# Retention attention and a squared-ReLU FFN on one core: four value loads on a second DMA queue, a new load order, other fillers

## The chip, the cores and the metric

The kernel runs on one core of a Trainium2 chip. A core has five engines that run side by side and wait for each other through semaphores: TensorE (PE, matrix products into PSUM), VectorE (DVE), ScalarE (ACT), GpSimd (POOL) and SyncE (SP, which here only issues DMA transfers). Weight loads of TensorE are listed apart as PEld. Sixteen DMA engines move data between HBM and SBUF; they are fed from queues of the issuing engines. The metric is the device time of one execution in microseconds, the median over several runs. The profile is taken from one execution; its span runs from the first to the last instruction.

## The reference

Two stages follow each other. The first is a recurrent attention with a decay per head; the second is an FFN with a squared ReLU.

```python
# q, k, v: (4, 8, 768, 64) f32; gamma_h = 1 - 2**(-5 - h)
for t in range(S):
    state = gamma * state + outer(k[:, :, t], v[:, :, t])
    y[:, :, t] = q[:, :, t] @ state / sqrt(D)
x = y.transpose(0, 2, 1, 3).reshape(3072, 512)
h = maximum(x @ w_in, 0)            # w_in 512 x 2048
out = (h * h) @ w_out               # w_out 2048 x 512, out 3072 x 512 f32
```

## The kernel before

The 3072 tokens are worked in 24 chunks of 128 tokens, six for each of four batches (`where(m)` gives batch and place). All eight heads of a chunk are worked together.

For each chunk `m`, `prepare(m)` loads k, q and v (256 KB each, in rows of 64 floats) into one of four staging slots, casts k and q to bf16, and scales v while casting it (L366). `transpose(m)` turns k and q, so that the head dimension lies on partitions: by TensorE through a PSUM bank (`T`, L408, with an eviction by ACT or DVE) for `m < NPE`, by small TensorE flips inside a visit (L381, one eviction at L387) for `NPE <= m < NTD`, and by a DMA transpose (L399) for the rest. `visit` holds the attention products of TensorE: scores (L451) and the chunk's own k-v sums (L462) for one chunk, values (L425) and the application of the state (L440) for another. DVE masks the scores (L505), updates the states (L516, L518) and writes the product with the decay factors to the activation tile `xt` (L527).

The FFN weights come in eight transfers of 1 MB: `i0` to `i3` are column quarters of w_in, `o0` to `o3` row quarters of w_out. They share four f32 staging buffers `wst`: `o0` uses the one of `i0`, and so on, so that a quarter of w_out can be loaded only when the casts of the same quarter of w_in are done. Each quarter is cast to bf16 in four slices, spread over DVE, ACT and POOL (`copy_on`, L341 to L345).

`ffn1(blk)` multiplies a block of one, two or four chunks (`BLOCKS`) with w_in: groups of 16, 8 or 4 matmuls of 128, 256 or 512 columns fill one of four PSUM banks `fps` (L565); ACT takes the ReLU (L570), DVE squares (L575). A group needs all chunks of its block and one quarter of w_in. `ffn2(blk)` multiplies each chunk's hidden layer with w_out (L608): 16 matmuls of 512 columns, in four pieces of four, one for each quarter of w_out, into one bank; at most two such groups are open at a time. ACT evicts the result (L616) and SyncE stores it (L620). Of the last chunk the output is worked in two halves of 256 columns.

The order of the instructions on all engines is made by a planner, `Plan.schedule`. It is a list scheduler with a model of durations: at each step it takes, over all engines, the operation that could start earliest, with the lowest `prio` among equals. The priority of a load is its place in the text `ORDER`; a store has -1, a DMA transpose -0.5. Operations with several possible engines (`CAST`, `WCAST`, `EVAC`) go where they start first. Loads are modelled as one shared pipe with a cost each (`SMALL`, `TURN`, `WIDE`, `STORE`), a number of descriptors against a ring limit of 198, and a time for which the issuing queue is held. The planned times only set the order; on the chip each instruction waits for its data.

TensorE gets filler matmuls that compute nothing used (L657): before each TensorE operation that is planned before `WARM`, as many as the planned idle time holds, times `FILL`. They write the last `fps` bank, which is withheld from other use until then. The priorities of F2 pieces contain `F2LAG`, in chunks, by which they stand behind the F1 groups.

All loads, transposes and stores are issued by SyncE.

Of the kernel before, what the change touches and what calls it, by code (L numbers as in the profile page):

```python
# [18 lines left out]
class Plan:  # L19
# [4 lines left out]


    DMA_LATENCY = 1.9
    LAND = 1.25
    RING = 198
    FETCH = 2.6
# [34 lines left out]
    def schedule(self, nbanks, max_open):  # L64
# [8 lines left out]
        start = [None] * n  # L73
        end = [None] * n
        eng_free = {}
        pool = {}
        for o in ops:
            for e in o["eng"]:
                eng_free.setdefault(e, 0.0)
                pool.setdefault(e, set())  # L80
                if left[o["i"]] == 0:
                    pool[e].add(o["i"])
        bank_free = [0.0] * (nbanks - 1) + [WARM]
        bank_of = {}
        open_groups = set()
        pipe = 0.0
        outstanding = {e: [] for e in eng_free}
        done = 0
        issued, edge, next_fetched, history, crossed = 0, self.BLOCK0, 3.0, [], 0.0
        while done < n:  # L90
            best = None
            for eng, cand in pool.items():
                ef = eng_free[eng]
                for i in cand:
                    o = ops[i]
                    t = max(ef, ready_at[i])
                    b = o["bank"]
                    if b is not None and b[0] == "open":
# [5 lines left out]
                        t = max(t, min(free))  # L104
# [5 lines left out]
            o = ops[i]  # L110
# [3 lines left out]
            dur = o["eng"][eng]  # L114
            move = isinstance(dur, tuple)
            if move:
                cost, n_desc, hold = dur
                out_ = outstanding[eng]
                while out_ and out_[0][0] <= t:
                    out_.pop(0)  # L120
                while sum(x[1] for x in out_) + n_desc > self.RING:
                    t = max(t, out_.pop(0)[0])
# [7 lines left out]
                    open_groups.add(b[1])  # L130
            if move:
                eng_free[eng] = t + hold
                pipe = max(pipe, t + self.DMA_LATENCY) + cost
                end[i] = pipe + self.LAND
                out_.append((pipe, n_desc))
                dur = hold
            else:
                if eng == "PE":
                    o["fill"] = 0
                    if t < WARM:  # L140
                        o["fill"] = int(max(0.0, t - max(eng_free[eng], 1.5) - 0.3) * FILL / 0.427)
                    issued += 2 * o["fill"]
                    todo, per = 2 * o["count"], dur / max(1, 2 * o["count"])
                    now = t
                    while issued + todo > edge:
                        step = max(0, edge - issued)
                        now = max(now + step * per, next_fetched)
                        issued, todo = max(issued, edge), todo - step
                        ahead = next((y for x, y in reversed(history) if x <= edge - self.AHEAD), 0.0)
                        ahead = max(ahead, crossed)  # L150
                        crossed = now
                        edge += self.BLOCK
                        next_fetched = ahead + min(5.7, max(0.3, pipe - ahead)) + self.FETCH
                    issued += todo
                    dur = now + todo * per - t
                    history.append((issued, t + dur))
                    o["dur"] = dur
                eng_free[eng] = t + dur
                end[i] = t + dur + o["lat"]
# [14 lines left out]
        return sorted(range(n), key=lambda i: (start[i], i))  # L174


SMALL = (1.20, 65, 0.6)
TURN = (1.10, 16, 2.4)
WIDE = (2.85, 33, 0.6)
STORE = (0.80, 9, 0.6)  # L180
BLOCKS = [1, 1, 1, 1, 1, 1, 2, 2, 2, 4, 4, 4]
SPLIT = 6
AHEAD = 4
WARM = 20.0
FILL = 0.8
PACE = 8
LEAD = 2
NPE = 6
NTD = 8
QACT = 0  # L190
F2LAG = 3.0
F2WAIT = 4
CAST = {"k": {"DVE": 0.43, "ACT": 0.63, "POOL": 0.78}, "q": {"DVE": 0.43, "ACT": 0.63, "POOL": 0.78}}
WCAST = {"DVE": 0.43, "ACT": 0.63, "POOL": 0.78}
# [2 lines left out]


ORDER = (
    "k0 q0 q1 v0 k1 q2 v1 k2 v2 v3 k3 q3 i0 i1 q4 o0 i2 i3 k4 o1 v4 o2 o3 v5 v6 q5 k5 q6 v7 q7 k6 k7"  # L200
)


# [8 lines left out]
def kernel(  # L212
# [9 lines left out]
    nc = tc.nc  # L222
    P = nc.NUM_PARTITIONS
# [22 lines left out]
    NBANK = 4  # L246
# [7 lines left out]
    ident = sb("ident", [P, P], BF16)  # L254
# [8 lines left out]
    ld = {x: sb(f"{x}n", [P, NLD, H * D], FP32) for x in "qkv"}  # L263
# [20 lines left out]
    pl = Plan()  # L284
# [63 lines left out]
    def prepare(m):  # L348
        b, i = where(m)
        slot = m % NLD  # L350
        for x in "kqv":
            t = ld[x][:, slot, :]
            side = x == "q" and m < QACT
            pl.add(f"ld{x}{m}", "ACT" if side else "SP", SMALL, (), (f"ld{x}{slot}",),
                   lambda x=x, t=t, q_=nc.scalar if side else nc.sync: q_.dma_start(  # L355
                       t.rearrange("s (h d) -> s h d", h=H),
                       src[x][b, :, i * C : (i + 1) * C, :].rearrange("h s d -> s h d")),
                   prio=dma_prio[(x, m)] - 200 * side)
        for x in "kq":
            t, o = ld[x][:, slot, :], bf[x][m % NBF]  # L360
            pl.add(f"c{x}{m}", CAST[x], 0, (f"ld{x}{slot}",), (f"bf{x}{m % NBF}",),
# [227 lines left out]
    def ffn2(blk):  # L589
        for q4 in range(blk0[blk], blk0[blk] + blocks[blk]):  # L590
# [5 lines left out]
            for part in range(parts):  # L596
# [4 lines left out]
                for j in range(4):  # L601
                    reads = [f"h{g % NH2}.{u}.{4 * j + c}" for c in range(4)] + [f"wout{j}.{c}" for c in range(4)]

                    def mm(j=j, o1=o1, h2=h2, u=u, ns=ns, w=w):
                        ps = fps[o1["op"]["bank_index"]]
                        for c in range(4):
# [1 line left out]
                            nc.tensor.matmul(ps[:, 0:w], lhsT=h2[:, fb, u * C : u * C + C], rhs=w_out_bf[j][:, c, ns],  # L608
                                             start=(fb == 0), stop=(fb == NFB - 1))
                    i0 = pl.add(f"F2.{q4}.{j}" + f"/{part}" * (parts > 1), "PE", 0.866 / parts, reads, (f"g{grp}",), mm,  # L610
                                prio=(q4 + F2LAG) * 8 + 2 * j + 1 + part * 0.5, lat=0.2,
                                bank=("open", grp, True) if j == 0 else ("use", grp), count=4)
                    if j == 0:
                        o1["op"] = pl.ops[i0]
# [37 lines left out]
    if tc is not None:  # L652
        with tc.manual_schedule():
            for i in sequence:
                o = pl.ops[i]
                for _ in range(o.get("fill", 0)):
                    nc.tensor.matmul(fps[NBANK - 1][:], lhsT=ident[:],  # L657
                                     rhs=ident[:, None, :].to_broadcast([P, 4, P]), start=True, stop=True)
                o["fn"](o["on"]) if o["flex"] else o["fn"]()
    return pl  # L660

# [29 lines left out]
```

## Time and profile before

| | |
|---|---|
| median of five runs | 215.99 us (214.99 to 216.83) |
| the profiled execution | 216.83 us |
| its span | 214.8 us |
| TensorE busy | 203.1 us, 95% |
| DVE, ACT, POOL busy | 53%, 41%, 20% |
| F1 matmuls (L565) | 768, 94.5 us busy |
| F2 matmuls (L608) | 400, 92.2 us busy |
| fillers (L657) | 12, 6.5 us busy |
| loads of k, q, v | 24 each, 256 KB each |
| weight loads | 8, 1 MB each, some 10.3 us from issue to landing |
| DMA transposes | 16 |

Busy times of TensorE overlap, since matmuls are pipelined: the busy sum is more than the time that the work takes in a row. In the list of pieces of the chain, each piece has its start, its length, engine, what and line. In the timeline, a line has start, length, engine, source line, operation, output and input, and in brackets how long the engine was idle before it and what ended that. A row of a stretch has the stretch, its length, the busy time and count of PE, PEld, DVE, ACT and POOL, the granted TensorE clock, the DMA share and the rate in GB/s. "SPq" is SyncE's queue, with the time in which it was occupied with issuing.

### The profile page before, as it was taken

The numbers are of one execution on the slowest core, as the hardware profiler recorded it, in microseconds if no ns is written. First come the engines' busy times: TensorE is split into PE (matmuls) and PEld (weight loads), VectorE is DVE, ScalarE is ACT, GpSimd is POOL, SyncE is SP. The second block draws the span as 40 slices with busy tenths as digits, with TensorE's granted clock in tenths as the row PEclk, the third lists the DMA queues.
The fourth block names the chain that finished last, engine by engine and source line by source line (L and its number), as shares of the span: only waits on it lengthen the run. The fifth ranks groups of instructions, "written<-read, shape, count | busy, mean of one in ns | idle before, by whom it ended". The sixth has DMA issues, their size and how long they took to land.

```text
span 214.8 us, 6317 instructions
## 1 busy us (share of the span) xinstructions
PE 203.1 (95%) x2764; PEld 121.2 (56%) x2764; DVE 113.1 (53%) x249; ACT 87.5 (41%) x145; POOL 42.1 (20%) x68
## 2 busy tenths in 40 slices
PE   6884899999999999999999999999999999999992
PEld 2453799776457787666754444454444444444461
DVE  1566767765149597675755665556554433322100
ACT  8222458735145254343331644223534324534211
POOL 5412323324331223132221223231100000000000
PEclk9999999999999999999999999999999999999999
DMA  7999999999899999989999999999811010011031
GB/s 142 216 203 331 352 348 319 346 244 231 203 268 187 190 182 194 236 194 210 236 199 236 206 218 167 221 202 170 153 50 52 3 63 34 3 49 49 28 112 56
DMA packets 99627, 38.15 MB, mean 178 GB/s; under 512 B 92304, under 2 KB 92560, under 8 KB 99600
## 3 DMA queue, kind: packets, MB, share of 16 engines
q1 hardware_dynamic: 99600, 37.76, 81.9%
q8 instruction: 21, 0.34, 0.7%
q14 instruction: 6, 0.05, 0.1%
HBM read 27.26 MB, written 6.29 MB: 156 GB/s over the span
## 4 chain that ended last, share of the span: by engine, by line
PE 83%; SPq 7%; DMA 5%; ACT 1%; issue 1%; DVE 1%; POOL 0%; ACTq 0%
PE fps L565 39%; PE fps L608 37%; SPq L355 7%; DMA wst<-in_moe_w_in_dram 3%; DMA qkT<-kqs 2%; PE yy L425 2%; PE yy L440 2%; PE sc L451 1%; PE sc L462 1%; ACT qkT L387 0%; PE fps L408 0%; POOL w_in L345 0%; ACT osb L616 0%; PE yy L381 0%; DVE xt L527 0%
## 5 line engine op out<-in xcount | busy, mean ns | idle before, releaser
L565 PE MATMUL fps<-xt,w_in 128*128 128x128 bf16 (+2 forms) x768 | 94.5, 278 | 1.2 <-POOL w_in L345 1.1
L608 PE MATMUL fps<-w_out,h 128*128 128x512 bf16 (+1 forms) x400 | 92.2, 371 | 0.0
L570 ACT ACTIVATE h<-fps 128x512 bf16<-128x512 f32 x96 | 57.3, 597 | 74.7 <-PE fps L565 74.7
L565 PEld LDWEIGHTS <-w_in 128*128 128x128 bf16 x768 | 61.1, 101 | 29.6 <-POOL w_in L345 1.2
L575 DVE TENSOR_TENSOR h<-h 128x512 bf16<-128x512 bf16 x96 | 42.5, 448 | 51.1 <-ACT h L570 50.8
L608 PEld LDWEIGHTS <-h 128*128 128x128 bf16 x400 | 37.5, 98 | 36.8
L345 POOL CAST kqs<-kn 128x512 bf16<-128x512 f32 x24 | 16.6, 691 | 60.9 <-DMA kn<-in_k_dram 50.4
L616 ACT ACTIVATE osb<-fps 128x512 f32<-128x512 f32 (+1 forms) x25 | 14.5, 580 | 31.5 <-PE fps L608 30.4
L527 DVE TENSOR_TENSOR xt<-yy,yf 128x512 bf16<-128x512 f32 x24 | 16.5, 688 | 16.1 <-PE yy L440 13.1
L345 POOL CAST kqs<-qn 128x512 bf16<-128x512 f32 x24 | 16.8, 702 | 29.5 <-DMA qn<-in_q_dram 29.4
L366 DVE TENSOR_TENSOR vs<-vn,vf 128x512 bf16<-128x512 f32 x24 | 17.1, 714 | 4.7 <-DMA vn<-in_v_dram 4.7
L505 DVE TENSOR_TENSOR pt<-sc,cmask 128x512 bf16<-128x512 f32 x24 | 16.4, 683 | 5.3 <-PE sc L462 5.3
L518 DVE TENSOR_TENSOR state<-sc,state 128x256 bf16<-128x256 f32 x40 | 16.8, 420 | 0.7
L440 PE MATMUL yy<-qkT,state 64*64 64x64 bf16 x352 | 12.5, 205 | 0.5
L425 PEld LDWEIGHTS <-vs 64*64 64x64 bf16 x384 | 5.3, 113 | 7.7 <-issue 7.6
L408 PE MATMUL fps<-ident,kqs 128*128 128x128 bf16 x48 | 6.4, 278 | 3.1 <-POOL kqs L345 2.9
L451 PE MATMUL sc<-qkT 64*64 64x64 bf16 x384 | 7.9, 202 | 1.1 <-ACT qkT L341 0.7
L440 PEld LDWEIGHTS <-state 64*64 64x64 bf16 x352 | 7.8, 113 | 1.2 <-PE yy L440 1.2
L462 PE MATMUL sc<-vs,kqs 64*64 64x64 bf16 x352 | 7.9, 201 | 0.3 <-DVE vs L366 0.2
L341 ACT ACTIVATE qkT<-fps 128x512 bf16<-128x512 bf16 x6 | 3.6, 597 | 11.3 <-PE fps L408 11.3
L425 PE MATMUL yy<-pt,vs 64*64 64x64 bf16 x384 | 8.1, 205 | 0.0
L408 PEld LDWEIGHTS <-kqs 128*128 128x128 bf16 x48 | 3.9, 120 | 7.3 <-POOL kqs L345 6.7
(32 smaller groups left out, 55.4 us busy)
## 6 DMA issues: line engine op xcount, KB each, us to landing
kn<-in_k_dram SPq DMA_DIRECT2D x24, 256.0 KB, 5.3
qn<-in_q_dram SPq DMA_DIRECT2D x24, 256.0 KB, 5.0
vn<-in_v_dram SPq DMA_DIRECT2D x24, 256.0 KB, 5.1
out_dram<-osb SPq DMA_DIRECT2D x23, 256.0 KB, 2.9
wst<-in_moe_w_in_dram SPq DMA_DIRECT2D x4, 1024.0 KB, 10.4
wst<-in_moe_w_out_dram SPq DMA_DIRECT2D x4, 1024.0 KB, 10.3
qkT<-kqs SPq DMA_TRANSPOSE x16, 4.9
out_dram<-osb SPq DMA_DIRECT2D x2, 128.0 KB, 2.1
```

The source lines that it names most:

```text
L345: nc.gpsimd.tensor_copy(o, t)
L355: lambda x=x, t=t, q_=nc.scalar if side else nc.sync: q_.dma_start(t.rearrange("s (h d) -> s h d", h=H), src[x][b, :, i * C : (i + 1) * C, ...
L366: lambda: nc.vector.tensor_tensor(out=o[:], in0=t.rearrange("s (h d) -> s h d", h=H), in1=vf[:, i, :, None].to_broadcast([P, H, D]), op=AL ...
L425: nc.tensor.matmul(yy[L * c : L * c + L, sub, p * L : p * L + L], lhsT=vs[r, 4 * a + j, :], rhs=pt[r, a, j, :], start=(p == 0), stop=True, ...
L440: nc.tensor.matmul(yy[L * c : L * c + L, sub, p * L : p * L + L], lhsT=st[r, j, :], rhs=qkT[r, 1, j, sub * L : sub * L + L], start=False, ...
L505: lambda: nc.vector.tensor_tensor(out=pt[:], in0=sc[:, :, 0:256].rearrange("s g (p t) -> s g p t", p=NJ), in1=cmask[:, None, None, :].to_b ...
L518: f = lambda cc=cc, j1=j1, j0=j0: nc.vector.tensor_tensor(out=sts[j1][:], in0=cc, in1=sts[j0][:], op=ALU.add)
L527: lambda: nc.vector.tensor_tensor(out=xt[:, :, u * C : u * C + C].rearrange("s p (g t) -> s g p t", g=2), in0=yy[:, :, 0:256].rearrange("s ...
L565: nc.tensor.matmul(ps[:, u * n : u * n + n], lhsT=w_in_bf[j][:, cb, c * P : (c + 1) * P], rhs=xt[:, cb, cols], start=(cb == 0), stop=(cb = ...
L570: nc.scalar.activation(h2[:, f0 : f0 + per, cols], ps[:].rearrange("p (u n) -> p u n", u=per), AF.Relu)
L575: nc.vector.tensor_mul(hv, hv, hv)
L608: nc.tensor.matmul(ps[:, 0:w], lhsT=h2[:, fb, u * C : u * C + C], rhs=w_out_bf[j][:, c, ns], start=(fb == 0), stop=(fb == NFB - 1))
```

## The change

The planner's model of a load gets two more quantities: a time for generating its descriptors (`gen`, with a latency `GEN_LATENCY`) apart from the time on the DMA engines. A load without descriptors in the ring (`SOFT`) stands for one issued by GpSimd.

- The loads of v for chunks 0 to 3 (`BYPOOL`) are issued by GpSimd, with a priority 50 lower than their place in `ORDER`; all other loads stay on SyncE.
- `ORDER` is new: weights stand earlier among the loads of k and q.
- `BLOCKS` is four blocks of two and four of four chunks, in place of six of one, three of two and three of four.
- `NPE` is 8, so chunks 6 and 7 are turned through `fps` banks and no flips in visits remain.
- Fillers are placed only in planned gaps of TensorE between `WARM - WARMING` (10.5) and `WARM + 1` (17) in the planner's time; each has 256 columns, not 512. The last bank is withheld until 17.
- `F2LAG` is 5 in place of 3.
- For the last chunk, the second half of the output gets a priority behind the whole first half; before, their pieces alternated.

```diff
+    GEN_LATENCY = 1.65
...
-        bank_free = [0.0] * (nbanks - 1) + [WARM]
+        bank_free = [0.0] * (nbanks - 1) + [WARM + 1]
...
-                cost, n_desc, hold = dur
+                gen, cost, n_desc, hold = dur
...
-                pipe = max(pipe, t + self.DMA_LATENCY) + cost
+                if n_desc:
+                    made = max(made, t + self.GEN_LATENCY) + gen
+                    ready = made + 0.15
+                else:
+                    ready = t + hold + 0.5
+                pipe = max(max(pipe, t + self.DMA_LATENCY) + cost, ready)
...
-                    if t < WARM:
-                        o["fill"] = int(max(0.0, t - max(eng_free[eng], 1.5) - 0.3) * FILL / 0.427)
+                    if WARM - WARMING < t < WARM + 1:
+                        o["fill"] = int(max(0.0, t - max(eng_free[eng], WARM - WARMING) - 0.1) / FILL)
...
-SMALL = (1.20, 65, 0.6)
-TURN = (1.10, 16, 2.4)
-WIDE = (2.85, 33, 0.6)
-STORE = (0.80, 9, 0.6)
-BLOCKS = [1, 1, 1, 1, 1, 1, 2, 2, 2, 4, 4, 4]
+SMALL = (1.20, 0.93, 65, 0.6)
+SOFT = (0.00, 0.93, 0, 1.8)
+TURN = (0.60, 1.10, 16, 2.4)
+WIDE = (0.60, 2.80, 33, 0.6)
+STORE = (0.30, 0.80, 9, 0.6)
+BLOCKS = [2, 2, 2, 2, 4, 4, 4, 4]
...
-WARM = 20.0
-FILL = 0.8
+WARM = 16.0
+FILL = 0.215
+WARMING = 5.5
...
-NPE = 6
+NPE = 8
...
-QACT = 0
-F2LAG = 3.0
+BYPOOL = ('v0', 'v1', 'v2', 'v3')
+F2LAG = 5.0
...
-    "k0 q0 q1 v0 k1 q2 v1 k2 v2 v3 k3 q3 i0 i1 q4 o0 i2 i3 k4 o1 v4 o2 o3 v5 v6 q5 k5 q6 v7 q7 k6 k7"
+    "o0 q0 k0 v0 v1 k1 o1 q1 k2 q2 i0 q3 o2 k3 i1 i2 v2 q4 i3 k4 o3 q5 v3 q6 v4 k5 v5 k6 v6 q7 v7 k7"
...
-            side = x == "q" and m < QACT
-            pl.add(f"ld{x}{m}", "ACT" if side else "SP", SMALL, (), (f"ld{x}{slot}",),
-                   lambda x=x, t=t, q_=nc.scalar if side else nc.sync: q_.dma_start(
+            soft = f"{x}{m}" in BYPOOL
+            pl.add(f"ld{x}{m}", "POOL" if soft else "SP", SOFT if soft else SMALL, (), (f"ld{x}{slot}",),
+                   lambda x=x, t=t, queue=nc.gpsimd if soft else nc.sync: queue.dma_start(
...
-                   prio=dma_prio[(x, m)] - 200 * side)
+                   prio=dma_prio[(x, m)] - 50 * soft)
...
-                                prio=(q4 + F2LAG) * 8 + 2 * j + 1 + part * 0.5, lat=0.2,
+                                prio=(q4 + F2LAG) * 8 + 2 * j + 1 + part * 9, lat=0.2,
...
-                    nc.tensor.matmul(fps[NBANK - 1][:], lhsT=ident[:],
-                                     rhs=ident[:, None, :].to_broadcast([P, 4, P]), start=True, stop=True)
+                    nc.tensor.matmul(fps[NBANK - 1][:, 0 : 2 * P], lhsT=ident[:],
+                                     rhs=ident[:, None, :].to_broadcast([P, 2, P]), start=True, stop=True)
```

More of the change, by code (lines that the diff above doesn't have):

```diff
@@ L82, in schedule @@
                     pool[e].add(o["i"])
-        bank_free = [0.0] * (nbanks - 1) + [WARM]
+        bank_free = [0.0] * (nbanks - 1) + [WARM + 1]
         bank_of = {}
         open_groups = set()
-        pipe = 0.0
+        pipe = made = 0.0
         outstanding = {e: [] for e in eng_free}
```

## The prediction

> **What bounds the kernel now.** I read the engines' busy shares first, then the chain that ended last, then the SyncE queue's issues in order of time, and last the wait list and the stretches.
>
> ```profile
> PE 203.1 (95%) x2764; PEld 121.2 (56%) x2764; DVE 113.1 (53%) x249; ACT 87.5 (41%) x145; POOL 42.1 (20%) x68
> PE 83%; SPq 7%; DMA 5%; ACT 1%; issue 1%; DVE 1%; POOL 0%; ACTq 0%
> ```
>
> TensorE is the bound, but not from the start. The pieces of the chain show two regimes:
>
> ```profile
> 12.53 2.16 SPq L355
> 14.74 6.67 DMA wst<-in_moe_w_in_dram
> 21.46 0.88 POOL w_in L345
> 22.34 0.05 issue
> 22.39 3.59 PE fps L565 x32
> ...
> 29.46 7.15 PE fps L565 x128
> ...
> 199.55 10.84 PE fps L608 x64
> ```
>
> Up to 22.39 us the chain is transfers. From there to 210.39 us (199.55 + 10.84) it is TensorE but for 7 us, and even there TensorE waited only 0.4 us. So the end is: arrival of the first weights, plus 188.0 us of TensorE work, plus 4.4 us behind its last matmul (two evictions, a store, its landing).
>
> The transfers decide both when TensorE may start and whether it can go on. By stretches (the last three columns are granted clock, DMA share, GB/s):
>
> ```profile
> 2.00:14.00 12.00, 10.54 (x123) 5.04 (x121) 5.67 (x14) 5.45 (x9) 4.49 (x10) 1.00 1.22 220
> 18.00:22.00 4.00, 2.52 (x72) 1.84 (x72) 2.02 (x6) 1.76 (x3) 1.15 (x2) 1.00 1.05 395
> 22.00:46.00 24.00, 23.45 (x393) 20.47 (x394) 17.00 (x38) 13.66 (x25) 6.84 (x10) 1.00 1.09 336
> ```
>
> While only k, q and v move, the rate is 220 GB/s; with weights alone 395. The casts date the landings: k0 4.2, the sixth load (q2) 10.4, the twelfth (q3) 18.2, weight i0 21.4, the last weight o3 46.7 us. A small load is thus 1.25 us in the queue, (10.4 − 4.2)/5. From i0 to o3 lie 25.3 us with seven weights and four small loads (q4, k4, v4, v5): (25.3 − 4 × 1.25)/7 = 2.9 us a weight. The second queue slice shows SyncE issuing with no pause:
>
> ```profile
> 6.77 0.89 SPq L355 DMA_DIRECT2D vn<-in_v_dram  x1
> 7.70 1.11 SPq L355 DMA_DIRECT2D kn<-in_k_dram  x1
> 8.86 2.44 SPq L355 DMA_DIRECT2D vn<-in_v_dram  x2
> 11.34 1.14 SPq L355 DMA_DIRECT2D kn<-in_k_dram  x1
> ```
>
> **The change, part by part.** The profiled execution took 216.83 us, 2.03 more than its span of 214.8; the median of the runs is 215.99, 0.84 below it. I sum on the profiled execution and take the difference to the median.
>
> **Queues and order.** o0, first in the new list, can't go first: it shares staging buffer wst0 with i0 and waits for i0's four casts. On SyncE, i0 thus stands behind six small loads, not twelve: 10.4 + 3.2 (q3 to i0 before, 21.4 − 18.2) = 13.6 us, plus four times what a v on the other queue takes from the engines, s. No row shows a GpSimd-queue load. If the 1.22 share means full DMA engines, s = 1.25; if SyncE's issue is the limit, s = 0. The Trainium skill speaks against the change here: "DMA: Bandwidth & Descriptors", section Issuing engines are not separate DMA queues, says that all issuers end on the same 16 engines and a second one saves only issue time. The same skill's "Perfetto Trace Analysis" (DMA Optimizations) allows a gain where descriptor generation is the limit, seen as a solid issuing track. The solid SyncE rows at 220 GB/s, against 395 with weights, are nearer to the second; the full share keeps me from zero. I take s = 0.5, an estimate: i0 lands at 15.6 (by the first rule 18.6, by the second 13.6). F1 starts one cast later, as now (21.4 to 22.39): 16.6, **5.8 us earlier**.
>
> GpSimd's cost: four generations, behind its constants, which end at 2.9. Its nearest row, a cast of the same tile, is 0.61 us; SyncE issues a load in 1.1; the diff's own plan holds the queue 1.8. I take 1.8, POOL busy to 10.1. The six casts it did meanwhile (0.61 each) go to DVE (0.43) and ACT (0.6), busy 5.7 and 5.5 of the 12 us up to 14: hidden. A rule against it: "SBUF — State Buffer", section SBUF: two separate sides, says that DVE copies that use the shared port pair keep GpSimd from writing descriptors. The row nearest is a POOL cast beside DVE casts:
>
> ```profile
> 21.46 0.87 POOL L345 CAST w_in<-wst 128x512 bf16<-128x512 f32 x1 [2.57 <-DMA wst<-in_moe_w_in_dram]
> 29.38 0.61 POOL L345 CAST w_in<-wst 128x512 bf16<-128x512 f32 x1 [1.87 <-DMA wst<-in_moe_w_in_dram]
> ```
>
> 0.26 us more when they meet. Six moved DVE casts at 0.26 to 0.43 make v3 1.6 to 2.6 us later, some 14 us. It is needed with k3, which now comes behind i0 at 18: nothing by the rule, nothing by the row.
>
> **What takes the gain back: the weights behind i0.** q3 and k3 now stand behind i0, and the other transfers are as many as before. From i0 to o3 I count seven weights and five small loads (q3, k3, q4, k4, q5): 7 × 2.9 + 5 × 1.25 = 26.6, so o3 lands at 42.2, **4.5 us earlier**, cast by 43.2 (before, 47.7 in the same count). From 16.6 to 43.2, 26.6 us, the data that are there allow: F1 of chunks 0 to 3, 4 × 3.5 = 14.0 (a 128-column matmul is 7.15/128 = 0.056 us; 64 a chunk; blocks of two 1.75/16 = 0.109 for twice the width); F2 of two open groups times three of four weights, 6 × 0.86 = 5.2; attention some 2.2. In all 21.4: TensorE idles 5 us between weights, where it had none. Now what is left after o3: before, 210.4 − 47.7 = 162.7. Up to 47.7 it had done 292 F1 matmuls (4.56 chunks) and 20 F2; after, 4 chunks and 24. F1 left: 4 × 3.5 + 16 × 3.45 = 69.2 against 67.5; F2 left: 0.9 less. So 162.7 + 1.7 − 0.9 = 163.5, and the last F2 ends at 43.2 + 163.5 = **206.7**, 3.7 earlier.
>
> **Wider blocks.** Chunks 8 to 11 form one block of 512 columns, so F1 waits for chunk 11. TensorE's other work lasts from 43.2 for F1 of chunks 4 to 7, 14.0, F2 of 6.5 chunks, 22.4, attention 6.0: until 85.6. Chunk 11 comes late now:
>
> ```profile
> 87.05 0.32 PE L451 MATMUL sc<-qkT 64*64 64x64 bf16 x16 [0.41 <-DMA qkT<-kqs]
> ```
>
> With its values and product behind, some 89; 4.5 us earlier, 84.8. Bounds 0 and, if the stream gains nothing there, 3.5; I take 0.5.
>
> **Fillers.** Twelve matmuls of 0.63 us spread over 1.6 to 16 give way to as many 256-column ones as fit from 10.5 to 17 of the plan. The granted clock reads 1.00 all along, yet the first 32 F1 matmuls take 3.59/32 = 0.112 us each and later ones 0.056. "TensorE: Matmul & The Clock Gate", Part 1, asks for about 3.4 us of sustained work; 6.5 us would do, and save 1.8 us. I book none: b0's matmuls on i0 end before i1 is there, so it falls into the idle 5 us. If the cover is gone, it is worth 1.8.
>
> **Chunks 6 and 7** turn by fps groups, 4 × 0.22, in place of flips, 2 × 0.38: +0.1, inside the rounding. F2LAG only orders work that is there.
>
> **Last output.** Both halves end together now, and their evictions run one behind the other:
>
> ```profile
> 210.46 0.38 ACT osb L616
> 210.84 0.00 issue
> 210.85 0.38 ACT osb L616
> ```
>
> With part 1 entirely behind part 0 (16 matmuls at 0.109, 1.7 us), one eviction remains: −0.4, at most −0.8 with its store's issue. Tail 4.0.
>
> **Sum:** 206.7 + 0.5 + 4.0 = span 211.2, 3.6 less; execution 213.2; against the median **212.4 us**.
>
> **Rivals.** *TensorE stays fed* (0.20): the order lets weights and chunks meet so that no idle comes. Then 188.0 − 1.8 (clock) − 0.6 (fewer narrow matmuls) + 1.0 (attention of chunk 3, done ahead before) = 186.6 from 16.6: 203.2 + 4.0 = 207.2, median 208.4. For it: no TensorE wait on weights but 1.1 us now. Against: DMA share above 1 up to 46 us.
>
> *The second queue brings nothing* (0.20): s = 1.25, o3 three us later, 215.4; within 0.5%, which is about what a measurement of this kernel can tell from no change.
>
> *Descriptor generation is slow, and the kernel slower* (0.13): at g us each, POOL is free at 2.9 + 4g; behind it stand k3's and q3's casts (1.2) and a slice of i0 (0.87). F1 needs that slice, and SyncE stops at o0 for it, with i3, k4 and the other weights queued behind. From 5.0 + 4g = 16.6, g = 2.9, it costs; past g = 4.1, 4.7 us, it outweighs my 3.6 and the 0.5%. At g = 5 it costs 8.4: 220.8. No row excludes it; the 1.1 us issue speaks against.
>
> *The forecast* has 0.47; its own range 210.4 (s = 0) to 214.9. The range 208.8 to 217.0 leaves out half of the first rival and the slow one, some 0.2. Faster: 0.42 of the forecast, 0.20, 0.06 of the second rival: 0.68. Slower: 0.13 and 0.02. Same: 0.17.
>
> **What would show it.** Right: first F1 near 16.6 with matmuls 0.056 apart; GpSimd loads of some 1.8 us; o3's casts near 42; TensorE gaps of 1 to 2 us between weights before 43; then none until the end except near 86; one eviction behind the last matmul. Wrong: i0 at 18 or later (s), F1 in one piece from its start (first rival), POOL solid beyond 14 us (third), or an F1 that stands at 0.11.

## The result and the profile after

The changed kernel takes **216.77 us** (median; 215.9 to 218.3) against 215.91 us of the kernel before on the same chips: ratio 1.0044, 95% interval 1.0033 to 1.0054. It is 0.9 us slower, where the forecast had it 3.6 us faster. The profiled execution of it took 216.28 us, 0.5 below its median, with a span of 214.3; that of before lay 0.8 to 0.9 above its median. So the two spans (214.3 and 214.8) make the changed kernel look 1.4 us better than the medians do; what is read below from pairs of traces has that uncertainty, and verdicts are taken from the medians.

The engines' busy shares and the shares of the chain of the changed kernel:

```profile
PE 197.4 (92%) x2461; PEld 108.9 (51%) x2461; DVE 115.4 (54%) x253; ACT 88.4 (41%) x148; POOL 41.3 (19%) x67
...
PE 56%; DMA 20%; SPq 18%; DVE 2%; issue 1%; POOL 1%; ACT 0%; POOLq 0%
```

TensorE had 83% of the chain before and has 56% now; DMA and SyncE's queue together went from 12% to 38%. The transfers hold the end further into the kernel than they did: the last transfer of the chain, and the first piece of TensorE behind it, are (start, length)

```profile
83.41 5.49 DMA vn<-in_v_dram
90.28 7.94 PE fps L573 x36
```

From 90.28 to its last matmul at 211.0 TensorE waits for nothing. In the kernel before, TensorE was on the chain from 22.39 on but for 7 us. The stretches say where (columns: stretch, length, busy time of PE, PEld, DVE, ACT, POOL, granted clock, DMA share, GB/s), first of the changed kernel, then the last one of before:

```profile
2.00:14.00 12.00, 4.32 (x67) 2.73 (x71) 4.98 (x12) 6.61 (x11) 5.21 (x9) 1.00 1.15 222
14.00:18.00 4.00, 2.89 (x66) 2.05 (x63) 1.64 (x4) 0.66 (x2) 0.64 (x2) 1.00 1.11 328
26.00:46.00 20.00, 19.43 (x180) 13.61 (x179) 14.99 (x32) 12.03 (x22) 7.71 (x10) 1.00 1.08 328
46.00:100.00 54.00, 52.92 (x860) 31.99 (x858) 34.90 (x73) 20.88 (x36) 12.99 (x20) 1.00 1.16 218
```

```profile
46.00:100.00 54.00, 53.53 (x942) 36.96 (x944) 34.40 (x69) 22.76 (x37) 15.56 (x22) 1.00 1.09 207
```

Up to 14 us the rate is 222 GB/s, with one queue it was 220: a second queue made the stream hardly faster. From 46 to 100 us, when only k, q, v, transposes and stores move, the DMA engines are nearly as full as at the start (share 1.16 and 1.09, against 1.15 and 1.22 up to 14 us). The transfers of 2 to 14 us by queue (packets, MB, share of 16 engines), after and before:

```profile
q1 hardware_dynamic: 6215, 1.61, 75.0%
q0 software_dynamic: 320, 1.05, 40.4%
```

```profile
q1 hardware_dynamic: 10403, 2.62, 121.1%
```

The GpSimd queue (q0) carries the four v in 320 packets, 3.3 KB each in the mean; SyncE's packets have 256 bytes. A MB costs 38.5% of the stretch there and 46.4% on SyncE's queue, so by the time of their packets the four v save (46.4 − 38.5) × 1.05 = 8% of 12 us, 1 us. That this becomes a gain isn't shown, since the rate up to 14 us is the same. The second queue is not a second road; what it gains comes behind 14 us, as the first experiment shows.

The start of the changed kernel in its timeline: the four loads issued by GpSimd, i0's first casts, the product of chunk 1, and the first F1:

```profile
3.06 3.77 POOL L363 DMA_DIRECT2D vn<-in_v_dram  x4
...
17.94 1.15 ACT L349 ACTIVATE w_in<-wst 128x512 bf16<-128x512 f32 x2 [0.88 <-DMA wst<-in_moe_w_in_dram]
...
19.71 0.68 DVE L535 TENSOR_TENSOR xt<-yy,yf 128x512 bf16<-128x512 f32 x1
...
20.45 1.03 PE L573 MATMUL fps<-xt,w_in 128*128 128x256 bf16 x8 [0.24 <-DVE xt L535]
```

A load costs GpSimd 3.77/4 = 0.94 us. i0 is there at 17.9, 3.5 us earlier than before (21.4). F1 starts at 20.45, 1.9 earlier, 2.5 us behind i0 where it was 1.0: it waits for `xt` of chunk 1, since the block has two chunks. Its matmuls are 0.11 us for 256 columns, the full pace, from the first on. Behind that TensorE has no idle time of 5 us between weights (1.6 us in all from 20 to 46 us), but more small waits than before, here three:

```profile
44.77 1.02 PE L616 MATMUL fps<-w_out,h 128*128 128x512 bf16 x4 [0.44 <-POOL w_out L353]
```

```profile
70.30 0.32 PE L459 MATMUL sc<-qkT 64*64 64x64 bf16 x16 [0.37 <-DMA qkT<-kqs]
```

```profile
90.28 1.04 PE L573 MATMUL fps<-xt,w_in 128*128 128x512 bf16 x4 [0.50 <-DVE xt L535]
```

The first is o3, the second a chunk's DMA transpose, the third the product of chunk 11. This product was not late by its own data: TensorE had done the values of chunk 11 by 87.9, but DVE, which works in its planned order, stood idle for 4.5 us up to 88.90, before the scaling of v of chunk 13, whose transfer is the one in the chain above. The last matmul ends at 211.0, one eviction follows:

```profile
211.06 0.38 ACT L624 ACTIVATE osb<-fps 128x256 f32<-128x256 f32 x1 [1.31 <-PE fps L616]
```

### The profile page after: what moved, and what is told of

Same layout as the page of the kernel before. It is cut to its first block, busy times and chain, and to the rows that moved or that the text cites. A ratio compares the mean times of both kernels' runs of the same rounds, so it can differ in the third digit from the quotient of the medians.

```text
span 214.3 us, 5724 instructions
## 1 busy us (share of the span) xinstructions
PE 197.4 (92%) x2461; PEld 108.9 (51%) x2461; DVE 115.4 (54%) x253; ACT 88.4 (41%) x148; POOL 41.3 (19%) x67
## 3 DMA queue, kind: packets, MB, share of 16 engines
q0 software_dynamic: 320, 1.05, 2.3%
## 4 chain that ended last, share of the span: by engine, by line
PE 56%; DMA 20%; SPq 18%; DVE 2%; issue 1%; POOL 1%; ACT 0%; POOLq 0%
PE fps L616 27%; PE fps L573 26%; SPq L363 12%; DMA vn<-in_v_dram 7%; SPq L549 5%; DMA kn<-in_k_dram 5%; DMA wst<-in_moe_w_out_dram 5%; DMA qn<-in_q_dram 2%; PE yy L433 1%; DVE vs L374 1%; PE yy L448 1%; PE sc L470 1%; PE sc L459 1%; SPq L407 1%; POOL kqs L353 1%
## 5 line engine op out<-in xcount | busy, mean ns | idle before, releaser
L573 PE MATMUL fps<-xt,w_in 128*128 128x256 bf16 (+1 forms) x512 | 90.8, 326 | 0.8 <-DVE xt L535 0.7
L616 PE MATMUL fps<-w_out,h 128*128 128x512 bf16 (+1 forms) x400 | 90.7, 371 | 0.4 <-POOL w_out L353 0.4
L573 PEld LDWEIGHTS <-w_in 128*128 128x128 bf16 x512 | 48.9, 98 | 35.1 <-DVE xt L535 1.0
L583 DVE TENSOR_TENSOR h<-h 128x512 bf16<-128x512 bf16 x96 | 41.6, 459 | 34.1 <-ACT h L578 34.0
L353 POOL CAST kqs<-kn 128x512 bf16<-128x512 f32 x22 | 14.4, 656 | 67.2 <-DMA kn<-in_k_dram 64.4
L353 POOL CAST kqs<-qn 128x512 bf16<-128x512 f32 x22 | 14.9, 677 | 17.5 <-DMA qn<-in_q_dram 17.1
L416 PE MATMUL fps<-ident,kqs 128*128 128x128 bf16 x64 | 7.6, 253 | 10.7 <-DVE kqs L351 5.1
L448 PE MATMUL yy<-qkT,state 64*64 64x64 bf16 x352 | 12.0, 199 | 0.5
L416 PEld LDWEIGHTS <-kqs 128*128 128x128 bf16 x64 | 4.8, 110 | 12.9 <-DVE kqs L351 5.3
L349 ACT ACTIVATE qkT<-fps 128x512 bf16<-128x512 bf16 x10 | 6.0, 597 | 12.2 <-PE fps L416 12.2
```

Of the source, the lines that this page charges most:

```text
L353: nc.gpsimd.tensor_copy(o, t)
L448: nc.tensor.matmul(yy[L * c : L * c + L, sub, p * L : p * L + L], lhsT=st[r, j, :], rhs=qkT[r, 1, j, sub * L : sub * L + L], start=False, ...
L573: nc.tensor.matmul(ps[:, u * n : u * n + n], lhsT=w_in_bf[j][:, cb, c * P : (c + 1) * P], rhs=xt[:, cb, cols], start=(cb == 0), stop=(cb = ...
L583: nc.vector.tensor_mul(hv, hv, hv)
```

## The experiments

**One part of the change undone.** First the queue: the four v back on SyncE, among the loads ahead of i0.

```diff
-BYPOOL = ('v0', 'v1', 'v2', 'v3')
+BYPOOL = ()
-    "o0 q0 k0 v0 v1 k1 o1 q1 k2 q2 i0 q3 o2 k3 i1 i2 v2 q4 i3 k4 o3 q5 v3 q6 v4 k5 v5 k6 v6 q7 v7 k7"
+    "o0 q0 k0 v0 k1 o1 q1 v1 k2 q2 v2 v3 i0 q3 o2 k3 i1 i2 q4 i3 k4 o3 q5 q6 v4 k5 v5 k6 v6 q7 v7 k7"
```

> The changed kernel with the four v loads back on SyncE, spread among the same ten loads ahead of i0. Theory 1 (the DMA engines are full with 256-byte rows, so the second queue adds nothing): i0 lands at 17.9 us within 0.7, as now, and the time is that of the changed kernel, 216.8 within 0.5. Theory 2 (SyncE's issue is the limit, and the second queue takes four loads off it): i0 lands at 4.15 + 9 x 1.25 + 3.2 = 18.6 or later, POOL's casts come earlier but F1 starts later, and the time is 217.5 or more.

Measured 219.31 us, ratio 1.0163 (1.0143 to 1.0184). i0 is cast from 19.08 on, against 17.94: with the second queue it came 1.1 us earlier there, 0.28 for each v. Up to 14 us the rate with one queue is no lower, 224 GB/s. What differs is the change from small loads to weights: in all seven traces with one queue a microsecond between 14 and 21 us has a DMA share of only 0.40 to 0.63, in none of the thirteen with two is it under 0.84. In the kernel before this is

```profile
15.00:16.00 1.00, 0.95 (x33) 0.38 (x24) 0.00 (x0) 0.00 (x0) 0.00 (x0) 1.00 0.59 126
```

That the hole is the gain, and the larger packets are not, fits these rows; no run separates the two. o3 is 2.1 us later, one more small load among them, and TensorE waits for it:

```profile
46.87 1.02 PE L616 MATMUL fps<-w_out,h 128*128 128x512 bf16 x4 [1.71 <-POOL w_out L353]
```

So the queue is worth 2.5 us at most within this order: the one more load ahead of o3 belongs to the new place of v2 and v3, and the granted clock was 0.50 from 18 to 22 us in this trace (1.00 in the changed kernel's), where the first eight F1 matmuls took 1.89 us in place of 1.03. "The second queue adds nothing" falls, though its share at i0 is a quarter of what a load takes.

Second, the blocks of before in the changed kernel, `BLOCKS = [1, 1, 1, 1, 1, 1, 2, 2, 2, 4, 4, 4]`; third, the halves of the last output alternating again, `part * 0.5`; fourth, `F2LAG = 3.0`.

> The changed kernel with the blocks of before (six of one chunk, three of two, three of four). Theory 3 (the lead of 2 us that TensorE has at 44 us is lost by 75 us because blocks of two and four wait for the last of their chunks): the lead stays, less 0.6 us for narrower matmuls, 215.4. Theory 4 (it is lost because the chunks themselves, k4 to v7, land no earlier than before, whatever the blocks): 216.8 to 217.4.

> The changed kernel with the pieces of the last two output halves alternating again. If one by one is worth what the two traces show behind the last matmul (4.0 against 3.3 us): 217.5. If the second store's landing sets the end anyway: 216.8.

> The changed kernel with the lag of the F2 pieces as before, 3 chunks in place of 5. By the theory that it only orders work that is there: no difference beyond 0.4 us, 216.4 to 217.2. The rival, that the longer lag lets F1 run ahead to blocks whose chunks are not there, while F2 that could fill the waits stands behind: the waits near 65 to 90 us (1.5 us together) go, and the time is 215.3 or so.

The narrow blocks: 219.86, ratio 1.0189 (1.0166 to 1.0212). The first F1 came 1.3 us earlier (19.14), and the time still rose by 3 us; the list of TensorE's waits has

```profile
PE sc L459 <- DMA qkT<-kqs: 2.5, 2, 1.6
```

at its head (us in total, times, longest): TensorE got to the late chunks before their transposes. The blocks of two are no loss here; that they make F1 wait for chunk 1 costs nothing that shows at the end. The halves: 217.03, 1.0060 (1.0030 to 1.0091), not separable from the changed kernel's 1.0044. The lag: 217.51, 1.0074 (1.0047 to 1.0101), no gain from 3; that the longer lag was a loss falls.

Fifth, the order of before (v0 to v3 still by GpSimd), and sixth the filler rule of before:

```diff
-    "o0 q0 k0 v0 v1 k1 o1 q1 k2 q2 i0 q3 o2 k3 i1 i2 v2 q4 i3 k4 o3 q5 v3 q6 v4 k5 v5 k6 v6 q7 v7 k7"
+    "k0 q0 q1 v0 k1 q2 v1 k2 v2 v3 k3 q3 i0 i1 q4 o0 i2 i3 k4 o1 v4 o2 o3 v5 v6 q5 k5 q6 v7 q7 k6 k7"
```

```diff
-                    if WARM - WARMING < t < WARM + 1:
-                        o["fill"] = int(max(0.0, t - max(eng_free[eng], WARM - WARMING) - 0.1) / FILL)
+                    if t < WARM:
+                        o["fill"] = int(max(0.0, t - max(eng_free[eng], 1.5) - 0.3) * FILL / 0.427)
```

> The changed kernel with the load order of before (v0 to v3 still on GpSimd): q3 and k3 come ahead of i0 again, v4 ahead of o2. The theory that the lead at the first F1 is what counts expects i0 two small loads later, some 20.2 us, the first F1 at 21.3 instead of 20.45, and the time 0.8 us longer, 217.6. The rival, that the new order is what takes the gain back (chunk 4 and 5 late, TensorE waits for o3's cast 0.6 us, for transposes and for chunk 11 another 1.5 us), expects the waits to go and the time 1 to 2 us shorter, 215.0 to 215.8.

> The changed kernel with the filler rule of before (twelve or so of 512 columns, from 1.5 us on). If the new fillers cost the changed kernel what they cost the kernel before (1.2 us), it comes to 215.6, on a par with the kernel before. If they earn the 1.8 us by which a cold clock lengthens the first 16 wide F1 matmuls (0.22 us each in place of 0.11), it goes to 218; if the stretch behind takes either back, as with halved loads, it stays at 216.8 within 0.4.

The old order: 218.27, 1.0101 (1.0070 to 1.0132). The new order isn't what loses within this kernel. The first F1 stood at 23.48, 3.0 us later than in the changed kernel, and the time was 0.57% longer (with an interval of some 0.33), 1.2 us: less than half of the lead at the first F1 is found at the end. The order behind it differs too, so this is no clean price of a lead. The old fillers: 217.08, 1.0043 (1.0021 to 1.0065), the same as the changed kernel, though the first F1 matmuls now ran at the slow pace:

```profile
20.46 1.86 PE L573 MATMUL fps<-xt,w_in 128*128 128x256 bf16 x8 [0.17 <-DVE xt L535]
```

From its start to that of the next piece it is 0.21 us a matmul in place of 0.11, 0.8 us lost on these eight; nothing of it is left at the end.

**One part alone in the kernel before.** The queue alone (`BYPOOL` with v0 to v3 added, order of before), the halves alone, the two together, the fillers alone (`WARM = 21.0`, `FILL = 0.215`, `WARMING = 5.5`, 256 columns), the blocks alone, and queue, halves and blocks together:

```diff
+BYPOOL = ('v0', 'v1', 'v2', 'v3')
-            pl.add(f"ld{x}{m}", "ACT" if side else "SP", SMALL, (), (f"ld{x}{slot}",),
+            pl.add(f"ld{x}{m}", "POOL" if soft else "SP", SOFT if soft else SMALL, (), (f"ld{x}{slot}",),
```

```diff
-BLOCKS = [1, 1, 1, 1, 1, 1, 2, 2, 2, 4, 4, 4]
+BLOCKS = [2, 2, 2, 2, 4, 4, 4, 4]
```

> The kernel before with one thing of the change alone: v of chunks 0 to 3 on the GpSimd queue, everything else (order, blocks, fillers) as before. From the comparison of two kernels that differ in the queue (i0 1.1 us later with one queue, 2.5 us longer in time) the theory that the second queue is a gain by itself expects i0 at 20.3 us in place of 21.4, the first F1 near 21.3, and the median 1.1 us below the kernel before, near 214.6. The rival, that the stretch up to the last weight is bound by bytes, so that an earlier i0 only moves a wait behind it, expects i0 early but o3 at 46.7 as before and a time within 0.4 us of the kernel before. A third, that GpSimd's generation delays its casts, expects i0's last cast late and a time over 216.3.

> The kernel before with the second output half behind the whole first half, nothing else. Prediction's step: 0.4 to 0.8 us less, 215.2; if the last store alone sets the end, no difference.

> The kernel before with two parts of the change: v of chunks 0 to 3 on the GpSimd queue, and the last output's halves one by one. If the two add (0.6 and 0.2 us): 215.1. The halves lie behind the last matmul and no stream can take them back: the sum should hold within 0.3.

> The kernel before with the fillers of the change alone, placed in planned gaps between 15.5 and 22 of the plan, 256 columns each. The first F1 matmuls of before stood 0.112 us apart, later ones 0.056: if the warm clock at i0 is worth its whole size, the first 32 matmuls take 1.8 us in place of 3.6, and the median falls by 1.8 to about 214.0. If TensorE only waits the longer for i1, which lands at 25.5 us and is cast by 26.4, then what there is to do on i0 alone (four groups for each chunk that is there) decides: a fall of at most 0.5 us, to 215.3 or more. If fillers delay the first transposes and attention: above 216.

> The kernel before with the blocks of the change alone (four of two and four of four chunks). In the changed kernel narrow blocks cost 3.1 us. If wide blocks are worth that by themselves, the median falls to some 213. On TensorE alone 384 narrow matmuls (0.056) for 192 of double width (0.109) save 0.6 us, to 215.3. If a block of two makes the first F1 wait for chunk 1 and chunk 11's block comes late at 86 us without the earlier stream, it is slower, 216.5 or more.

> The same two parts and the wide blocks too, with the load order and fillers of before. If wide blocks are worth 0.6 us by themselves: 214.5, the best of all. If they need the other load order, above 216.

| in the kernel before | us | ratio | interval |
|---|---|---|---|
| queue | 215.61 | 0.9973 | 0.9957 to 0.9989 |
| halves | 215.57 | 0.9989 | 0.9974 to 1.0005 |
| queue, halves | 215.70 | 0.9984 | 0.9969 to 0.9998 |
| fillers | 217.10 | 1.0054 | 1.0035 to 1.0073 |
| blocks | 222.06 | 1.0268 | 1.0242 to 1.0295 |
| queue, halves, blocks | 221.69 | 1.0259 | 1.0237 to 1.0281 |

The queue alone is a gain, of 0.2 to 0.9 us, half of what was expected; the halves gain a little or nothing, and the two together are not more than the queue: the sum of 0.8 us was not found. i0 was expected at 20.3 us. In the three traces with queue and the old order its first cast on GpSimd is at 20.96, 21.55 and 21.35, within what six traces of that order with one queue have (20.81 to 21.81; the one of before 21.46): no gain at i0. At o3 there is one: 45.24 to 45.30, against 45.65 to 46.73, in the mean 0.85 us, of which 0.3 to 0.6 is found in the time. The three kernels with queue or halves are the fastest that were run with the whole computation, and the intervals do not rank them.

Fillers and blocks alone were expected to gain or do nothing, and both lose. The fillers did what they are for: the first 32 narrow matmuls took 2.07 us in place of 3.59. Then, some 57 us later, this:

```profile
80.79 0.32 PE L452 MATMUL sc<-qkT 64*64 64x64 bf16 x16 [1.46 <-DMA qkT<-kqs]
```

The blocks alone cost 6 us. Their list of waits begins with

```profile
PE fps L565 <- DVE xt L527: 2.6, 1, 2.6
PE fps L608 <- POOL w_out L345: 1.8, 1, 1.8
```

The first is at 61.7: TensorE has run out of F1 and F2 and stands before a block of two until its second chunk is there; in the timeline it does little else than two visits from 56.4 on. So undoing the wide blocks in the changed kernel costs 3 us, and adding them to the kernel before costs 6. That they need the new order (the chunks' k and q ahead) is not the reason, or not the whole one: the changed kernel with the order of before has wide blocks, queue and halves too and takes 218.27, where these parts in the kernel before take 221.69. Between those two stand fillers, `F2LAG`, `NPE` and the planner's costs; which of them makes the 3.4 us was not run. The granted clock was below 1 in parts of the two slow traces (0.83 and 0.71 from 60 to 70 us), which may have its share.

**A lighter stream.** The theory left was that the transfers from 46 to 100 us, at 207 to 218 GB/s with the DMA engines full, set when chunks are ready, so that a lead of TensorE turns into waits there. To test it, v of chunks 6 to 17 brings half of its heads, in three kernels, with the planner's costs and so the orders left as they are:

```diff
+            n = H // 2 if x == "v" and 6 <= m < 18 else H
-                       t.rearrange("s (h d) -> s h d", h=H),
-                       src[x][b, :, i * C : (i + 1) * C, :].rearrange("h s d -> s h d")),
+                       t.rearrange("s (h d) -> s h d", h=H)[:, 0:n, :],
+                       src[x][b, 0:n, i * C : (i + 1) * C, :].rearrange("h s d -> s h d")),
```

> The kernel before, in which the v loads of chunks 6 to 17 bring only half of the heads (128 KB in place of 256; the other half is stale, so part of the attention is left out of the loads, not of the arithmetic). The order of instructions is the same. If the DMA engines, full from 46 to 100 us, are what TensorE runs into, the 7 us of transfers taken out end the wait at 86 us (0.58) and what little else waits there: 0.6 to 1.0 us shorter, 215.0. If waits come from SyncE's order and issue, not from bytes: within 0.3 us of the kernel before.

> The kernel before with the new fillers, and v of chunks 6 to 17 loaded by half (leaves out half of these loads). With whole loads it had a lead of 1.5 us from 26 to 60 us and lost it in waits for DMA transposes at 62.7, 67.6 and 78.9 (2.5 us together). If full DMA engines take the lead back, it keeps it here: 1.3 to 1.8 us below the kernel before with halved loads, some 213.5. If the lead is lost by the planner's order, the waits stay and it is 1 us above that kernel, 216 or more.

> The changed kernel with v of chunks 6 to 17 loaded by half (leaves out half of these loads). By the theory of full DMA engines its lead in work done (2.1 us at 44 us, of which 0.7 go in the wait for o3, which stays) is kept: 1 us below the kernel before with halved loads, some 214.2. By the theory that the change only adds TensorE work (transposes behind the first F1, attention not done ahead, 2 us) and the waits count for little, it stays 0.5 to 1 us above that kernel, 216.

| | whole loads | halved | interval of the halved |
|---|---|---|---|
| before | 1 | 0.9955 (215.16 us) | 0.9937 to 0.9973 |
| before with new fillers | 1.0054 | 0.9958 (215.26) | 0.9945 to 0.9971 |
| changed | 1.0044 | 0.9945 (214.89) | 0.9927 to 0.9963 |

The kernel before gains 0.45%, 1.0 us; the two with a lead at the first F1 gain 0.96% and 0.99%, 2.1 us each. Their whole deficit is gone. The stretch from 46 to 100 us goes the same way, for the changed kernel with halved loads (its row with whole loads stands above, 52.92 us busy), for the fillers with whole and with halved loads, and for the kernel before with halved loads (with whole loads 53.53):

```profile
46.00:100.00 54.00, 53.92 (x869) 32.74 (x867) 36.91 (x76) 22.06 (x38) 13.60 (x22) 1.00 1.15 207
```

```profile
46.00:100.00 54.00, 51.87 (x934) 35.78 (x933) 34.21 (x71) 21.18 (x35) 13.80 (x23) 1.00 1.11 213
```

```profile
46.00:100.00 54.00, 53.88 (x950) 37.13 (x948) 35.76 (x73) 22.33 (x37) 15.52 (x24) 1.00 1.12 205
```

```profile
46.00:100.00 54.00, 53.70 (x939) 37.04 (x939) 33.90 (x69) 22.75 (x37) 15.29 (x22) 1.00 1.05 183
```

TensorE is busy 1.0, 2.0 and 0.2 us more of the 54. These figures alone prove little: the kernel with the halves alone, which differs from before only in the last chunk, has 52.52 here. The waits are firmer. In the changed kernel those for the DMA transpose at 70.30 and for chunk 11 at 90.28 are gone; the product of chunk 11 is written from 87.2 on, and its F1 block starts at 88.64, 1.6 us earlier, as much as the last matmul is earlier (209.4 against 211.0). The expected size was missed all the same: both were to end 1 us or more below the kernel before with halved loads, and are level with it. So the stream took back what made them slower, some 1.1 us, and not the whole gain of the forecast. The halved loads are those of v, one of which holds up chunk 11; whether lighter loads of k or q would do the same was not run. A halved load has half the packets as well as half the bytes; whether the bytes or the packets fill the engines these runs do not tell.

**More loads on the second queue.** If the queue saves 0.28 us a load, twelve or four more might relieve the stream. In the changed kernel v6 to v17 with the low priority of the first four; then in both kernels v4 to v7 at their place in the order (`- 50 * (soft and m < 4)`), in the kernel before together with queue and halves.

> The changed kernel with v of chunks 6 to 17 on the GpSimd queue as well. The first four each saved 0.28 us of the stream on SyncE's queue. By the theory of full DMA engines twelve more save up to 3 us of the transfers between 46 and 100 us, the waits at 65, 70 and 87 us go, and the time is 1 us shorter, 215.8. If GpSimd's four casts per chunk wait behind generations (0.94 us each) or behind a slot that isn't free, kqs is late, the DMA transposes with it: 218 or more.

> The changed kernel with v of chunks 4 to 7 on the GpSimd queue too, at their place in the order and not ahead of it. In the run with twelve more such loads GpSimd stood behind loads whose buffers were not free (12.3 us of waits), and kqs and weight slices were late behind it. If that, and not the queue itself, was the trouble, four more loads at their place save 0.28 us of the stream each: o3 some 0.5 us earlier, chunks 5 to 7 up to 1 us, and the time falls by 0.3 to 1.0, to 216.2. If any load in GpSimd's order holds its casts up: 217.5 or more.

> The kernel before with v of chunks 0 to 7 on the GpSimd queue (4 to 7 at their place), and the last output's halves one by one. TensorE waited little there (1.5 us in all from 46 to 125 us), so four more loads on that queue can bring 0.3 us at most over the same kernel with four: 215.3. If GpSimd's casts are held up: 216.5 or more.

Twelve more: 1.0472 (1.0413 to 1.0532), 226.9 us (median of three). Four more: 1.0231 (1.0198 to 1.0263) in the changed kernel, 1.0180 (1.0150 to 1.0210) in the kernel before. All are losses, and the last run shows why. GpSimd issues v4 to v7 as soon as their buffers are free, and i0's slice is cast at 25.95:

```profile
9.93 0.89 POOL L357 DMA_DIRECT2D vn<-in_v_dram  x1 [0.92 <-DVE vs L368]
12.29 0.88 POOL L357 DMA_DIRECT2D vn<-in_v_dram  x1 [1.46 <-DVE vs L368]
14.28 0.88 POOL L357 DMA_DIRECT2D vn<-in_v_dram  x1 [1.10 <-DVE vs L368]
...
16.99 0.89 POOL L357 DMA_DIRECT2D vn<-in_v_dram  x1
```

```profile
26.88 1.35 PE L567 MATMUL fps<-xt,w_in 128*128 128x128 bf16 x11 [2.98 <-POOL w_in L347]
```

i0 stands in SyncE's queue, but that order binds only SyncE's transfers: four loads of GpSimd passed it, and it landed at 25.9, 4.5 us later than before, some 1.1 us for each. The first F1 at 26.88 is 4.5 us later than in the profile of before, and the time 3.9 us longer. TensorE then waited for no transpose at all.

## Why the prediction was wrong, step by step

**What bounds the kernel** was half right. That the start is set by transfers held, and it went on longer: the chain of the changed kernel leaves them at 90.28. The forecast took everything behind o3 as TensorE's own, but for one wait at 86. The stretch 46 to 100 had DMA engines nearly as full as the first 14 us (share 1.09 against 1.22); that row was not read.

**Queues and order.** The forecast took s, what a v on the other queue takes from the engines, as 0.5, between 0 and 1.25. Measured: i0 at 17.9, so (17.9 − 13.6)/4 = 1.08, nearly a whole load. The rule that was weighed and set aside, in the Trainium skill's "DMA: Bandwidth & Descriptors", Issuing engines are not separate DMA queues, was right in substance: up to 14 us the rate is 222 GB/s against 220. The row that I judged it by, SyncE issuing without pause at 220 GB/s and 395 with weights, showed full engines holding the issuing up, not the issuing holding the engines up; the DMA share of 1.22 in the same line said so. A whole load for each v would have given i0 at 18.6; whether the 0.7 us between are the larger packets or the hole that is missing with two queues is not shown.

GpSimd's generation was put at 1.8 us and took 0.94; that nothing waited for its casts held.

**The first F1** was to start one cast behind i0, at 16.6. It started at 20.45: 2.3 us from s, and 1.5 because a block of two waits for chunk 1's product, which the forecast did not price. With the narrow blocks it stood at 19.14. Since the sum was anchored at o3, this error cost the sum nothing; it only did away with the idle 5 us, so that TensorE was little short of work between the weights (1.6 us).

**The weights behind i0** is the step that failed. o3's last cast is at 44.8, not 43.2: 1.6 us, from s. (The trace of before, from which the 4.5 us were counted, also has the latest o3 of six traces of that order with one queue, 46.7 against 46.1 in the mean.) What was done by then was exactly as counted, 128 F1 matmuls (four chunks) and 24 F2. But in the difference of the work left behind o3 only F1 and F2 had been counted, the attention and transposes not. The matmuls of the transposes and of the values in the stretch from o3's cast to the end (44.77 after, 47.70 before):

```profile
44.77:214.00 169.23, 1.96 (x20) 1.29 (x20) 1.00 0.79 149
```

```profile
47.70:214.00 166.30, 0.77 (x8) 0.61 (x8) 1.00 0.77 150
```

```profile
44.77:214.00 169.23, 6.37 (x320) 4.15 (x320) 1.00 0.79 149
```

```profile
47.70:214.00 166.30, 6.04 (x304) 3.96 (x304) 1.00 0.77 150
```

Twelve transposes (0.67 us at 0.056 each) and one chunk's attention (0.65) are left that had been done earlier before; the flips of chunks 6 and 7 that fall away give back 2 × 0.28. The forecast had 164.0 us from o3's cast to the last matmul, the 0.5 for chunk 11 included; it was 211.0 − 44.8 = 166.2. Where the 2.2 us lie shows against the path that the forecast wrote out in its next step, from o3's cast to the F1 block of chunks 8 to 11. From the starts of TensorE's pieces between 44.77 and 90.28:

| | forecast | measured |
|---|---|---|
| F1 of chunks 4 to 7 | 14.0 | 14.3 |
| F2 (6.5 chunks; measured 6.25) | 22.4 | 22.7 |
| attention and transposes | 6.0 | 7.7 |
| waits | 0.5 | 0.9 |
| in all | 42.9 | 45.5 |

So 2.6 us are lost here, 1.7 of them by attention and transposes, which were put too low. Behind 90.28 come 120.8 us, where the forecast had 121.1. Together 1.6 + 2.6 − 0.3, some 3.8 us: TensorE ended at 211.0, not at 207.2.

**Wider blocks**: a wait of 0.5 us for chunk 11 was forecast at about 86, and is there, 0.50 at 90.3. Its size is luck, two misses of like size: TensorE came to this block at 89.8, not 85.6, and chunk 11's product was there at 90.2, not 84.8. The scores of chunk 11 did come 4.8 us earlier than before (82.25 against 87.05), as forecast. But its values stand behind 20 F2 matmuls in TensorE's order, at 87.11, and its product behind v of chunk 13 on DVE; in the kernel before, too, its values came at 91.1 and the product not at some 89. What the step lacked besides is that other chunks come late: waits of 0.1 at 65 and 0.4 at 70 in this trace, and 0.8 to 1.5 us for transposes in those of three of the kernels with one part undone (halves, lag, fillers). The halved loads put the price of this stream at 1.1 us of the kernel's time (2.1 us less with them, against 1.0 in the kernel before; the intervals leave 0.5 to 1.7).

**Fillers**, booked at nothing and at 1.8 us if the cover is gone: nothing within the change is what the old rule showed (1.0043 against 1.0044). In the kernel before they are a loss of 1.2 us, outside both bounds, since the lead ran into the stream.

**Last output**: −0.4, at most −0.8. One eviction is left behind the last matmul, as said; in the kernel before it brings 0.2 us, with an interval that holds nothing and 0.6.

**The sum** had a span of 211.2; 214.3 was measured. The 3.8 us of TensorE are lessened by a tail of 3.3 in place of 4.0, which is luck: it comes from a last store that landed sooner (1.7 us after its issue against 2.6). The other 1.3 us of the miss, from the spans to the medians, is how the two profiled executions stand to their medians.

**The rivals.** "TensorE stays fed" was right that no 5 us of idle time came, and wrong in its time, as it kept the start at 16.6. "The second queue brings nothing" has s nearest to the measured one, and its 215.4 is nearest of the rivals; still undoing the queue in this order costs 2.5 us, part of it by what moves with it. "Generation is slow" falls with 0.94 us. The mechanism that made the kernel slower, a later stream that turns the lead into waits, was in none of them.

What stays open: after the stream is made lighter, the changed kernel is level with the kernel before although its first F1 is 1.9 us earlier. Transposes, attention and the wait for o3, 1.1 to 1.4 us, would cover most of it; no run shows it, and the remainder is not settled.

## What to carry to other kernels

Before a lead at the start is booked as a gain at the end, read the DMA share of every later stretch too: as long as the engines stay full behind it, TensorE can catch up with its inputs and hand the lead back as waits, here at 65 to 90 us for a lead made at 20. Look also at what stands ahead of a product in its own engine's order: chunk 11 was held up by a load for chunk 13. A second queue is no second road: it takes its share from the first and passes what stands there, so put on it only what is needed sooner than everything on the other. When work is counted as "left after" a point, count all of an engine's kinds of work, also the small ones that were done ahead before.

## What the runs showed of the hardware

- The GpSimd queue sends these loads (rows of 256 bytes) in packets of 3.3 KB in the mean, SyncE in packets of 256 bytes, and a MB takes 17% less packet time of the DMA engines (38.5% and 46.4% of the same 12 us). The rate did not rise with it (222 and 220 GB/s). A generation for 1024 such rows takes GpSimd 0.94 us; a load lands 7.6 us after its issue, where SyncE's took 5.1 in the stretch of before, and 8.0 (k) and 10.0 (q) beside it.
- A transfer of the GpSimd queue passes one that waits in SyncE's: four loads made i0 4.5 us later. The Trainium skill ("DMA: Bandwidth & Descriptors", SWDGE vs HWDGE vs iDMA) says that the engines take turns between the queues of the two; that agrees with it.
- The granted clock reads 1.00 from 20 to 22 us in the changed kernel with the old fillers and in the changed one, yet the same eight matmuls took 1.86 and 1.03 us; with one queue it reads 0.50, and they took 1.89. The column did not show the slow pace of the first of these; the interval between matmuls did.
- The last store landed 1.7 us after its issue in the changed kernel, and 2.6 in the kernel before, also with its halves one by one; in the kernel before with queue and halves it took 1.7. No run explains it.
